# One memset instead of two behind some gathers, and three merge operations ahead of the last sums: a sort-based GraphSAGE aggregation on one core

## The chip, the cores and the metric

The kernel runs on one core of a Trainium2 chip. A core has TensorE (PE: matrix products, and PEld, the weight loads beside them), VectorE (DVE), ScalarE (ACT), GpSimd (POOL) and SyncE (SP), which run their own instruction streams and wait for each other through semaphores. 16 DMA engines move data between HBM and the core's memory. The metric is the device time of one launch in microseconds (us). Of the kernel before, three runs gave 2193.62, 2194.74 and 2198.55 us, so its median is 2194.74 us.

## The reference

A graph of 12,500 nodes and 800,000 edges is given as two index lists. Every node has 64 features. The features of the edges' sources are added up onto the edges' destinations, the sum is scaled by the inverse in-degree, and two 64x64 products give the output:

```python
N, deg, D = 12500, 64, 64
E = N * deg

def reference(x, src, dst, deg_inv, w_self, w_neigh):
    nsum = _segment_sum(x[src], dst, N)      # tgt.at[dst].add(x[src])
    h_neigh = nsum * deg_inv[:, None]
    return x @ w_self + h_neigh @ w_neigh
```

`src` and `dst` are drawn at random, so the gather and the scatter are irregular. The kernel turns them into a sort and dense products.

## The kernel before, in words

Every edge becomes one 32-bit key: a bucket number (block of 144 destinations x block of 128 sources), then the destination and the source inside the block. The program then goes through these stages.

1. **Sort in each partition.** Each of the 128 partitions sorts its 6,250 keys on DVE (line 228), and the result `runs` is written to memory as `d1`. This takes the first quarter of the time.
2. **First run gathers.** The buckets are given to 128 + 128 rows: part 0 (41 buckets a row) and part 1 (27 a row). `find_rows` counts on ACT and DVE where each row's run begins in each partition, and `gather_runs` (line 468) fetches, for each of the 128 partitions p, one short run per row: an indirect DMA on POOL's queue, with `start[part]` as the indices. There are 128 such gathers for part 0 (`range(128)`), then 104 for part 1 (`FIRST = 104`), and later 24 more. Behind every gather stands `pause()` (line 382): two memsets on POOL of a scratch tile `pad` that nothing reads then.
3. **Merges.** `merge_runs` merges the gathered runs of a row on DVE by min and max operations (lines 280 and 292; ACT copies what stays, line 276). Part 0 is merged in groups of 16, 16, 32 and 64 runs, so the last group's first operation needs gathers 64 to 127. `merge_last` (lines 309 to 324) makes the last level of part 0.
4. **Counts.** `find_buckets(0)` counts on ACT, for each of the 41 buckets of a row, how many keys lie below it (line 605). When the last count is there, two small DVE operations (lines 621 and 622, the "last sums") make the start of every bucket's window.
5. **Bucket gathers.** `gather_buckets(0)` makes the index of each window (line 637, DVE) and fetches it (line 626, POOL, an indirect DMA into `v`), with a `pause()` behind each of the 41. Behind them POOL runs the last 24 run gathers of part 1.
6. **Decode.** `decode_buckets(0)` splits the gathered keys, four buckets at a time, into source and destination (lines 673 to 678 on DVE, 683 and 687 on ACT, a transpose on PE).
7. **Nodes.** For every bucket, DVE makes a one-hot matrix of the sources (`ohs`, line 780, from a DMA `slb` that spreads the indices over the partitions) and one of the destinations (`ohd`, line 783). PE multiplies (`ct`, line 808), ACT, and from the second half on DVE too, copies the product out of PSUM (`xg`, lines 818 and 816), and PE adds up with `ohd` (`acc`, line 864). 1,066 tiles of 8 buckets go through this. Part 1's merges, its find, gather and decode run between the tiles.

The order on every engine is written by hand: the whole of `after_sort` and `sums_and_merge` stands in one `manual_schedule` block, and instructions are issued on each engine in the order in which Python emits them. Merges of part 1 are a generator whose steps are pulled one by one. Steps are pulled where the program wants DVE to have work: two bucket counts per merge step while the counts last (`while counts:` in `sums_and_merge`), then some 8 us of merges by an estimate, then 2.8 us of them per decode step, and in the nodes stage 0.32 us per tile.

Of the kernel before, what the change touches and what calls it, by code (L numbers as in the profile page):

```python
# [31 lines left out]
KPRS = (41, 27)  # L32
# [21 lines left out]
SPLIT = 2560  # L54
SIGMA = 6.0
LOWER = 2240
LAG = 4
OCT = 7

# [47 lines left out]
WIN = Windows()  # L107
NLOWER = sum(lo + n <= LOWER for lo, n in WIN.w2[0])
NC1 = len(WIN.w1)
# [189 lines left out]
def merge_last(nc, src, oth, off, rstride, ln, lout, split, done):  # L299


    plan, na, nb, alone = merge_plan(ln, lout)

    def at(t, z, n):
        return view(t, off + z, [[2, n]])

    for op, n, z in ((OP.min, na, 0), (OP.max, nb, 1)):
        x, y = (view(src, off + o, [[1, n]]) for o in (0, rstride))
        nc.vector.tensor_tensor(at(oth, z, n), x, y, op=op)
        yield n / 0.96 + 125  # L310
    for a, e in alone:
        z = 2 * (a % ln) + a // ln
        nc.scalar.activation(at(src, z, e - a), at(oth, z, e - a), AF.Copy)
    edge = [split]
    for (first, *_), (then, *_) in zip(plan[-2::-1], plan[:0:-1]):
        edge.insert(0, edge[0] + max(2 * first - 1, 2 * then - 1))
    for upper in range(2):
        cur, nxt = oth, src
        for (k, lo, *ends), e in zip(plan, edge):
            for op, end, z in zip((OP.min, OP.max), ends, (1, 2 * k)):  # L320
                i = max(0, -((z - e) // 2))
                a, b = (max(lo, i), end) if upper else (lo, min(end, i))
                if b > a:
                    nc.vector.tensor_tensor(at(nxt, 2 * a + z, b - a), at(cur, 2 * a + 1, b - a),
                                            at(cur, 2 * (a + k), b - a), op=op)
                yield (b - a) / 0.96 + 125
            cur, nxt = nxt, cur
        if not upper:
            done(cur)


def flat(ap, n):
    return bass.AP(tensor=ap.tensor, offset=ap.offset, ap=[[1, n], [1, 1]])


class Kernel:
# [39 lines left out]
        nc.gpsimd.iota(self.wide, pattern=[[1, OCT * HN]], base=0, channel_multiplier=0,  # L376
                       allow_small_or_imprecise_dtypes=True)

    def pause(self):

        for _ in range(2):
            self.nc.gpsimd.memset(self.pad, 0.0)  # L382

    def make_keys(self, pool, keys):
# [78 lines left out]
    def gather_runs(self, part, u, runs):  # L463
        nc = self.nc
        nr, w = ROWS[part], LENS[part][0]
        src = flat(self.d1, 128 * PITCH1)
        for p in runs:
            nc.gpsimd.indirect_dma_start(  # L468
                out=u[:nr, p * w:(p + 1) * w], out_offset=None, in_=src,
                in_offset=bass.IndirectOffsetOnAxis(ap=self.start[part][:nr, p:p + 1], axis=0))  # L470
            self.pause()

    def merge_runs(self, part, u, pong, sizes):

# [7 lines left out]
        def round_(level, off, rstride, nruns):  # L482
            src = bufs[par[level]]
            args = nc, src, bufs[1 - par[level]], off, rstride
            if part == 0 and level == 6:
                def done(rows):
                    self.rows, self.lower = rows, True
                yield from merge_last(*args, lens[level], lens[level + 1], LOWER, done)
            else:
# [120 lines left out]
    def find_buckets(self, part):  # L610


        nc = self.nc
        acc = self.keep.tile([128, KPRS[part]], F32, name=f"acc2_{part}")
        nc.sync.dma_start(self.d2[part][:, SIDE:SIDE + LOWER], self.rows[:, :LOWER])
        for k in range(KPRS[part]):
            if k == NLOWER:
                nc.sync.dma_start(self.d2[part][:, SIDE + LOWER:SIDE + LROW[part]], self.rows[:, LOWER:LROW[part]])
            self.count_below(part, k, acc)
            yield k  # L620
        nc.vector.tensor_tensor(acc, acc, self.c2[part][:, 3], op=OP.mult)
        nc.vector.tensor_tensor(acc, acc, self.c2[part][:, 4], op=OP.add)
        self.first = acc
# [6 lines left out]
    def gather_buckets(self, part, vp):  # L630

        nc = self.nc
        kpr = KPRS[part]
        self.v = vp.tile([128, kpr, 2 * SIDE], I32, name="v")
        ix = self.keep.tile([128, kpr], U32, name=f"ix2_{part}")
        for k in range(kpr):
            nc.vector.tensor_scalar(ix[:, k:k + 1], self.first[:, k:k + 1], 0.0, None, op0=OP.max)
            self.gather_window(part, k, ix)
            self.pause()

    def find_and_gather(self, part, vp):

# [5 lines left out]
        ix = self.keep.tile([128, kpr], U32, name=f"ix2_{part}")  # L648
        for k in range(kpr + LAG):
            if k == 1:  # L650
                self.store_rows(part, nc.scalar)
            if k < kpr:
                self.count_below(part, k, acc)
            if k >= LAG:
                g = k - LAG
                nc.scalar.activation(ix[:, g:g + 1], acc[:, g:g + 1], AF.Relu, bias=self.c2[part][:, 4, g:g + 1])
# [504 lines left out]
```

## Time and profile before

| what | before |
|---|---|
| median of the runs shown | 2194.74 us (2193.62 to 2198.55) |
| profiled execution | 2187.01 us, span 2185.2 us |
| busy: PE, DVE, ACT, POOL | 1031.3, 1998.6, 1261.8, 651.4 us |
| line 228, in-partition sort on DVE | 228.5 + 227.3 us |
| lines 808 and 864, products on PE | 602.7 + 411.1 us |
| line 468, run gathers on POOL | 256, 339.1 us busy |
| line 382, pauses on POOL | 594 memsets, 114.7 us busy |

The profiled execution is one run, 7.7 us below the median of the others. The page shows busy time per engine, the program's lines with their counts and mean durations, and what each engine waited for. A timeline row gives start, duration, engine, line, operation, the tiles written and read, and in brackets the idle time just before with the releaser that ended it. An engine's busy share over the whole span says little here, because the stages follow each other with different engines in the lead. DVE leads up to about 1090 us, and from there PE, DVE and ACT are all nearly full.

### The profile page before, as it was taken

Reading aid. Unit: us, or ns where it says so; the run is one execution under the profiler, and the core shown is the slowest. Engines: PE = TensorE matmul, PEld = TensorE weight load, DVE = VectorE, ACT = ScalarE, POOL = GpSimd, SP = SyncE. Lnnn points to the kernel's source line nnn. Section 1 sums busy time; section 2 is a strip of 40 time slices with the busy share of each in tenths; the row PEclk is TensorE's granted clock in tenths of the full one; section 3 lists DMA queues with packets and bytes.
Section 4 is the critical chain, followed back from the end, with each engine's and each line's share of the span. In section 5 each row is a group of like instructions: output and inputs, shape, how many; then the busy total and the mean of one; then the engine's idle time right before and its main releaser. Section 6 shows DMA issues by size and latency. Waiting matters only on the chain.

```text
span 2185.2 us, 59787 instructions
## 1 busy us (share of the span) xinstructions
PE 1031.3 (47%) x26089; PEld 888.8 (41%) x26089; DVE 1998.6 (91%) x2198; ACT 1261.8 (58%) x1747; POOL 651.4 (30%) x1020
## 2 busy tenths in 40 slices
PE   0150000000000000000089998999987989999987
PEld 0140000000000000000077887877776878788776
DVE  7999999999899599988999999999998888889887
ACT  6470000019500000062289999999997888888886
POOL 1000000001888888977861100101431010010010
PEclk9965555555555555555589999999999999999999
DMA  5140000000000000012188777778876887777784
GB/s 159 37 107 6 0 0 0 0 24 39 21 19 20 16 14 13 10 53 57 50 293 280 272 284 265 270 270 278 310 271 219 291 272 291 263 279 291 277 280 163
DMA packets 111311, 331.46 MB, mean 152 GB/s; under 512 B 56528, under 2 KB 64656, under 8 KB 110400
## 3 DMA queue, kind: packets, MB, share of 16 engines
q1 hardware_dynamic: 90352, 306.14, 38.9%
q0 software_dynamic: 14864, 19.18, 4.8%
q8 instruction: 206, 3.38, 0.6%
q10 hardware_dynamic: 5824, 2.24, 0.4%
q14 instruction: 65, 0.53, 0.1%
HBM read 308.39 MB, written 19.10 MB: 150 GB/s over the span
## 4 chain that ended last, share of the span: by engine, by line
PE 35%; DVE 28%; POOL 18%; issue 10%; ACT 7%; DMA 3%; another core or an unknown queue 0%; ACTq 0%; SPq 0%; DVEq 0%; POOLq 0%
PE ct L808 20%; PE acc L864 13%; POOL u L468 13%; DVE a L228 10%; DVE b L228 9%; POOL pad L382 4%; ACT xg L818 2%; ACT junka L449 2%; DVE ohd L783 2%; DVE ohs L780 2%; DVE u L292 1%; DMA v<-d,ix 1%; PE po L932 1%; POOL v L626 1%; PE acc L869 1%
## 5 line engine op out<-in xcount | busy, mean ns | idle before, releaser
L818 ACT ACTIVATE xg<-ct 128x1024 f16<-128x1024 f32 (+1 forms) x994 | 937.8, 1082 | 102.6 <-PE ct L808 83.4
L808 PE MATMUL ct<-xh,ohs 128*128 128x128 f16 x8526 | 602.7, 222 | 49.9 <-DVE ohs L780 20.1
L808 PEld LDWEIGHTS <-ohs 128*128 128x128 f16 x8526 | 498.6, 99 | 96.6 <-issue 35.8
L468 POOL DMA_INDIRECT u<-d,ix x256 | 339.1, 1325 | 533.7 <-ACT junka L449 491.2
L292 DVE TENSOR_TENSOR u<-u 128x256 f32<-128x256 f32 (+47 forms) x494 | 453.3, 949 | 23.7 <-ACT u L276 15.8
L864 PE MATMUL acc<-ohd,xg 64*128 64x72 f16 x17052 | 411.1, 194 | 57.0 <-issue 42.2
L864 PEld LDWEIGHTS <-xg 64*128 64x128 f16 x17052 | 324.6, 95 | 133.0 <-issue 52.5
L780 DVE TENSOR_SCALAR ohs<-slb,pidx 128x3584 f16<-128x3584 bf16 x305 | 350.5, 1149 | 24.3 <-PE ct L808 18.9
L783 DVE TENSOR_TENSOR ohd<-iota,dlT 128x2016 f16<-128x2016 bf16 x305 | 366.6, 1202 | 0.0
L693 PE MATMUL tr<-idb,l 128*128 128x128 bf16 x68 | 9.0, 271 | 493.4 <-ACT l L687 488.5
L228 DVE TENSOR_TENSOR a<-b 128x106 f32<-128x106 f32 (+31 forms) x114 | 228.5, 2056 | 1.2
L228 DVE TENSOR_TENSOR b<-a 128x106 f32<-128x106 f32 (+36 forms) x112 | 227.3, 2080 | 1.0
L276 ACT ACTIVATE u<-u 128x256 f32<-128x256 f32 (+15 forms) x94 | 46.8, 577 | 310.2 <-DVE u L280 309.0
L693 PEld LDWEIGHTS <-l 128*128 128x128 bf16 x68 | 5.6, 117 | 496.9 <-ACT l L687 492.3
L458 PE MATMUL stp<-idf,st 128*128 128x128 f32 x2 | 0.9, 446 | 416.0 <-DVE st L456 416.0
L940 POOL DMA_DIRECT2D out<-o x24 | 24.7, 1029 | 547.5 <-DVE o L939 518.9
L458 PEld LDWEIGHTS stp<-idf,st 128*128 128x128 f32 x2 | 0.4, 182 | 416.5 <-issue 416.5
L845 POOL DMA_INDIRECT lx<-xt,lxi x44 | 78.9, 1793 | 300.0 <-PE ct L808 161.0
L816 DVE CAST xg<-ct 128x1024 f16<-128x1024 f32 x75 | 91.7, 1223 | 57.1 <-PE ct L808 57.0
L231 ACT ACTIVATE a<-b 128x106 f32<-128x106 f32 (+12 forms) x20 | 13.5, 708 | 205.2 <-DVE b L228 198.6
L382 POOL MEMSET pad<- 128x89 f32 x594 | 114.7, 193 | 17.5
L280 DVE TENSOR_TENSOR u<-u 128x512 f32<-128x512 f32 (+21 forms) x68 | 75.8, 1145 | 26.5 <-DMA u<-d,ix 22.8
(135 smaller groups left out, 858.2 us busy)
## 6 DMA issues: line engine op xcount, KB each, us to landing
slb<-sl SPq DMA_DIRECT2D x305, 896.0 KB
u<-d,ix POOLq DMA_INDIRECT x256
xt<-xh SPq DMA_DIRECT2D x1, 3136.0 KB
own<-os SPq DMA_DIRECT2D x12, 256.0 KB
fo<-own SPq DMA_DIRECT2D x24, 126.0 KB
out<-o POOLq DMA_DIRECT2D x24, 126.0 KB
rd<-dst SPq DMA_DIRECT2D x4, 521.0 KB
rs<-src SPq DMA_DIRECT2D x4, 521.0 KB
```

The costliest lines, as they stand in the source:

```text
L228: nc.vector.tensor_tensor(view(dst, lo + sh, [[st, g], [1, l]]), x, y, op=op)
L280: nc.vector.tensor_tensor(at(oth, to, n), x, y, op=op)
L292: nc.vector.tensor_tensor(to, at(cur, ln + lo, n), at(cur, lo + k, n), op=op)
L382: self.nc.gpsimd.memset(self.pad, 0.0)
L468: nc.gpsimd.indirect_dma_start(out=u[:nr, p * w:(p + 1) * w], out_offset=None, in_=src, in_offset=bass.IndirectOffsetOnAxis(ap=self.start[ ...
L780: nc.vector.tensor_scalar(s.rearrange("p c s -> p (c s)"), b, self.pidx[:, :1], None, op0=OP.is_equal)
L783: nc.vector.tensor_tensor(d, self.iota[:, None].to_broadcast([128, 14, HN, 2]), ix, op=OP.is_equal)
L808: nc.tensor.matmul(ct[:, i * 128:(i + 1) * 128], cols[i][0], self.xh[:, (b0 + i) % NB].rearrange("p a f -> p (a f)"), start=True, stop=True)
L816: nc.vector.tensor_copy(xg[:, :cnt * 128], ct[:, :cnt * 128])
L818: nc.scalar.activation(xg[:, :cnt * 128], ct[:, :cnt * 128], AF.Copy)
L845: nc.gpsimd.indirect_dma_start(out=x, out_offset=None, in_=self.xt, in_offset=bass.IndirectOffsetOnAxis(ap=ix.bitcast(U32), axis=0))
L864: nc.tensor.matmul(acc[h][:, db % OCT * HN:(db % OCT + 1) * HN], xg[r, i * 128:(i + 1) * 128], d[r], start=db % OCT == 0 and sb == 0, stop ...
```

## The change

`pause` takes a number of memsets. Gathers 32 to 127 of part 0 and the 41 bucket gathers get one memset instead of two; gathers 0 to 31 of part 0 and all gathers of part 1 keep two. And `find_buckets` yields six more times between the last count and the last sums. Since two steps of it are pulled per merge step, three merge operations of part 1 come to stand ahead of the two sums in DVE's order, and all later merge operations stand three steps earlier in the program.

```diff
+CLOSE = 32
+BEHIND = 6
...
-    def pause(self):
-
-        for _ in range(2):
+    def pause(self, n):
+
+        for _ in range(n):
             self.nc.gpsimd.memset(self.pad, 0.0)
...
                 in_offset=bass.IndirectOffsetOnAxis(ap=self.start[part][:nr, p:p + 1], axis=0))
-            self.pause()
+            self.pause(1 if part == 0 and p >= CLOSE else 2)
...
             self.count_below(part, k, acc)
             yield k
+        for _ in range(BEHIND):
+            yield KPRS[part]
         nc.vector.tensor_tensor(acc, acc, self.c2[part][:, 3], op=OP.mult)
         nc.vector.tensor_tensor(acc, acc, self.c2[part][:, 4], op=OP.add)
...
             self.gather_window(part, k, ix)
-            self.pause()
+            self.pause(1)
```

On POOL nothing moves: 137 of its 594 memsets are gone, 96 behind gathers 32 to 127 of part 0 and 41 behind the bucket gathers. In the changed kernel lines up to `find_buckets` lie two lower (468 becomes 470, 382 becomes 384), later ones four.

DVE's order around the last sums (`acc`), which wait for ACT's last count, before:

```order
L292 TENSOR_TENSOR u<-u 128x32x40
L621 TENSOR_TENSOR acc_0_2196<-acc_0_2196,c_0_69 128x41
L622 TENSOR_TENSOR acc_0_2196<-acc_0_2196,c_0_69 128x41
L637 TENSOR_SCALAR ix_0_2318<-acc_0_2196 128x1 x41
L292 TENSOR_TENSOR u<-u 128x32x39
L292 TENSOR_TENSOR u<-u 128x32x40
L292 TENSOR_TENSOR u<-u 128x32x39
L280 TENSOR_TENSOR u<-u 128x16x80 x2
```

and with the change:

```order
L294 TENSOR_TENSOR u<-u 128x32x40
L294 TENSOR_TENSOR u<-u 128x32x39
L294 TENSOR_TENSOR u<-u 128x32x40
L294 TENSOR_TENSOR u<-u 128x32x39
L625 TENSOR_TENSOR acc_0_2100<-acc_0_2100,c_0_69 128x41
L626 TENSOR_TENSOR acc_0_2100<-acc_0_2100,c_0_69 128x41
L641 TENSOR_SCALAR ix_0_2225<-acc_0_2100 128x1 x41
L282 TENSOR_TENSOR u<-u 128x16x80 x2
```

The three merge operations that stood behind the 41 index operations now stand ahead of the sums.

In the nodes stage DVE alternates one-hot pairs (`ohs`, `ohd`) with merge operations of part 1. Its second group of 64 runs begins with the operation of 128x32x48. Before, it stands behind 13 one-hot pairs:

```order
L280 TENSOR_TENSOR u<-u 128x780
L292 TENSOR_TENSOR u<-u 128x485 x2
L292 TENSOR_TENSOR u<-u 128x689
L780 TENSOR_SCALAR ohs<-slb,pidx 128x3584
L783 TENSOR_TENSOR ohd<-iota,dlT 128x2016
```

These are the rows ahead of the first pair. With the change four later merge operations stand there, and the 128x32x48 stands behind 8 pairs:

```order
L294 TENSOR_TENSOR u<-u 128x733
L294 TENSOR_TENSOR u<-u 128x749
L294 TENSOR_TENSOR u<-u 128x733
L294 TENSOR_TENSOR u<-u 128x741
L784 TENSOR_SCALAR ohs<-slb,pidx 128x3584
L787 TENSOR_TENSOR ohd<-iota,dlT 128x2016
```

So the second group, which reads what the last 24 run gathers fetch, begins five one-hot pairs earlier.

## The prediction

> **What bounds the kernel now.** I read the busy times first, then a table by stage, then who waited for whom on DVE.
>
> ```profile
> PE 1031.3 (47%) x26089; PEld 888.8 (41%) x26089; DVE 1998.6 (91%) x2198; ACT 1261.8 (58%) x1747; POOL 651.4 (30%) x1020
> ...
> 530.00:735.00 205.00, 0.89 (x2) 0.36 (x2) 185.74 (x384) 58.41 (x210) 170.99 (x343) 0.50 0.08 19
> 735.00:757.00 22.00, 0.00 (x0) 0.00 (x0) 0.11 (x1) 0.00 (x0) 18.64 (x43) 0.50 0.09 21
> ...
> 975.00:1097.00 122.00, 7.69 (x54) 4.87 (x55) 109.72 (x183) 26.96 (x48) 94.22 (x169) 0.50 0.22 62
> 1097.00:1300.00 203.00, 190.51 (x4918) 164.01 (x4915) 200.24 (x222) 194.98 (x220) 48.78 (x36) 0.97 0.80 280
> ```
>
> In the rows of stretches the columns are start and end, length, then busy us of PE, PEld, DVE, ACT and POOL, the granted clock, the DMA share and GB/s. Up to 1097 us DVE carries the program and PE does almost nothing. From there PE, DVE and ACT are all over 93% busy, so that stage has a length of its own (2185 - 1097 = 1088 us) and follows whatever starts it. Between 735 and 757 every engine but POOL stands. What DVE waits for in the first half:
>
> ```profile
> DVE u L280 <- DMA u<-d,ix: 22.8, 1, 22.8
> DVE ohs L780 <- PE ct L808: 18.9, 23, 2.1
> ...
> DVE acc L621 <- ACT junk L605: 6.7, 1, 6.7
> DVE v L673 <- DMA v<-d,ix: 6.1, 6, 1.8
> ```
>
> The columns are the sum in us, how often, and the longest. The change is aimed at rows one, three and four: 22.8 + 6.7 + 6.1 = 35.6 us at most.
>
> **The run gathers (22.8 us).** The hole stands between these rows:
>
> ```profile
> 640.71 1.54 POOL L468 DMA_INDIRECT u<-d,ix  x1 [0.15 <-issue]
> ...
> 714.46 19.67 DVE L292 TENSOR_TENSOR u<-u 128x849 f32<-128x849 f32 x16 [1.73 <-ACT u L276]
> ...
> 738.34 0.42 POOL L382 MEMSET pad<- 128x89 f32 x2
> 738.92 0.95 POOL L468 DMA_INDIRECT u<-d,ix  x1 [0.15 <-issue]
> ...
> 754.19 0.95 POOL L468 DMA_INDIRECT u<-d,ix  x1 [0.15 <-issue]
> ...
> 756.89 4.49 DVE L280 TENSOR_TENSOR u<-u 128x2048 f32<-128x2048 f32 x2 [22.76 <-DMA u<-d,ix]
> ```
>
> DVE is through with three groups of runs at 714.46 + 19.67 = 734.13. The fourth needs gather 127, which POOL begins at 754.19 and ends at 755.14. DVE goes on 1.75 us later, when the data have landed. With DVE idle a gather takes 0.95 us, its two memsets 0.42 and the gap 0.15 (a pitch of 1.53). What one memset costs:
>
> ```profile
> 699.96 0.19 POOL L382 MEMSET pad<- 128x89 f32 x1
> ```
>
> So 0.42 - 0.19 = 0.23 us go per gather, and 0.34 instead of 0.57 us lie between two gathers. For 96 gathers that is 96 x 0.23 = 22 us, almost the whole hole, if POOL waits for nothing else. It does wait while DVE works:
>
> ```profile
> 721.71 1.93 POOL L468 DMA_INDIRECT u<-d,ix  x1 [1.55 <-issue]
> 722.73 7.68 DVE L292 TENSOR_TENSOR u<-u 128x1085 f32<-128x1085 f32 x6
> 724.04 1.30 DVE L292 TENSOR_TENSOR u<-u 128x1093 f32<-128x1093 f32 x1
> 724.22 1.95 POOL L468 DMA_INDIRECT u<-d,ix  x1 [0.15 <-issue]
> ...
> 726.75 1.95 POOL L468 DMA_INDIRECT u<-d,ix  x1 [0.15 <-issue]
> ...
> L468 POOL DMA_INDIRECT u<-d,ix x50 | 63.5, 1269 | 9.1 <-issue 9.1
> L382 POOL MEMSET pad<- 128x89 f32 x100 | 18.1, 181 | 2.9
> ```
>
> The gather that starts at 724.22 meets the DVE operation that ends at 724.04 + 1.30 = 725.34, and itself ends at 724.22 + 1.95 = 726.17, 0.83 later. A gather thus ends 0.95 us after its start or 0.83 us after the end of the DVE operation that it met, whichever is later. Memsets are not held up (181 ns each). The gathers 64 to 113 (x50) take 1.27 us on average for that reason. In the stretch of long operations POOL and DVE are locked in step: one gather for two operations (726.75 - 724.22 = 2.53 = 2 x 1.27). From 0.83 us behind an operation's end it is 0.34 us to the next start, 1.17 together, which is just short of one operation (7.68 / 6 = 1.28). So there the step should fall from two operations to one; with 0.57 us it is 1.40, over one. That is what decides this term.
>
> I went through all recorded starts and ends of DVE's operations with this rule, gather by gather from 32 on, with 0.34 us between gathers. (With 0.57 it gives back the recorded starts up to the 1.55 us gap at 721.71.) Gather 64 then starts at 635.0 and not at 640.71, and the last one at 735.4 and not at 754.19. The saving is **18.8 us**: 22 by count, less 5 of longer waits (the last 14 gathers no longer have an idle DVE), and 1.4 because the issue gap, which follows the number of instructions issued, falls behind gather 127. If the gap stays, it is 17.5. With 0.33 us between gathers the same gives 20.0, with 0.36 us 16.1. The low bound is that every gather which waited for DVE gives its saving back as a longer wait: 42 of the 96 took the bare 0.95 us (counted in the timeline), so 42 x 0.23 = 10 us. The high bound is the hole, 22.8. I take 18.8; DVE still waits 4 us.
>
> The Trainium skill ("SBUF — State Buffer", section "Who interferes with whom") says that a DVE instruction with two SBUF inputs contends with a GpSimd instruction that reads SBUF, not with one that only writes it. The trace agrees: gathers (which read their indices) wait, memsets do not. The page adds that the first to start holds the port for its whole instruction and the other fully blocks; what that would make of the time is the third rival.
>
> **The three merge operations (6.7 us).** They are these x3, and they fill a wait:
>
> ```profile
> 974.63 0.20 DVE L621 TENSOR_TENSOR acc<-acc,c 128x41 f32<-128x41 f32 x1 [6.71 <-ACT junk L605]
> 977.60 4.35 DVE L292 TENSOR_TENSOR u<-u 128x1248 f32<-128x1248 f32 x3
> ```
>
> 4.35 of 6.71 us are filled, and the sums still wait 2.4 us for ACT's last count; the bucket gathers start no sooner and no later against that count. Behind them the program pulls the same number of merge steps as before (8 us, then 2.8 per decode step), only later ones. So this part does not bring the nodes stage forward. It takes 4.35 us of DVE work out of it. PE, DVE and ACT share the lead there, so I book 0, with 4.35 as the best case.
>
> **The bucket gathers (6.1 us).**
>
> ```profile
> L626 POOL DMA_INDIRECT v<-d,ix x41 | 50.4, 1230 | 27.7 <-issue 14.1 <-DVE ix L637 7.2 <-DVE v L673 2.7
> 983.72 1.98 POOL L626 DMA_INDIRECT v<-d,ix  x1 [0.53 <-issue]
> 987.66 0.69 DVE L673 TENSOR_TENSOR v<-v,c 128x512 int32<-128x512 int32 x1 [1.80 <-DMA v<-d,ix]
> ```
>
> 41 gathers fill 976 to 1066 us, 2.2 us each, of which 0.95 lie between two gathers (0.42 + 0.53). DVE works off four in about 8 us, so it waits for them: 6.1 us in six waits, the first of 1.80. With 0.23 less per gather the last one ends 41 x 0.23 = 9.4 us sooner, less what DVE's operations hold up. By the same rule and the changed order of DVE, none of the six waits is left; with the old order the first would keep 1.5. I take **5.5 us**, bounds 0 and 6.1.
>
> **The nodes stage.** Its start moves by 18.8 + 5.5. One thing in it does not move along: the second group of part 1 now stands behind 8 one-hot pairs and not 13, and needs the last 24 run gathers.
>
> ```profile
> 1094.47 1.15 DVE L780 TENSOR_SCALAR ohs<-slb,pidx 128x3584 f16<-128x3584 bf16 x1 [1.59 <-DMA slb<-sl]
> ...
> 1114.54 10.58 POOL L468 DMA_INDIRECT u<-d,ix  x1 [0.15 <-issue]
> ...
> 1120.37 0.91 DVE L292 TENSOR_TENSOR u<-u 128x738 f32<-128x738 f32 x1
> ...
> 1128.83 0.95 POOL L468 DMA_INDIRECT u<-d,ix  x1 [0.15 <-issue]
> ...
> 1138.22 1.75 DVE L280 TENSOR_TENSOR u<-u 128x1536 f32<-128x1536 f32 x1
> ...
> L468 POOL DMA_INDIRECT u<-d,ix x9 | 24.8, 2753 | 1.4 <-issue 1.4
> ```
>
> Before, the last gather ends at 1129.8 and lands some 2 us later, 37 us behind the first one-hot; the merge needs it at 1138.22, 44 us behind. Eight pairs end at about 1120, so the need now comes 26 us behind the first one-hot. The last nine gathers, caught between one-hots, took 36 us with their memsets, 4 each; with the bucket gathers done 4 us sooner against the first one-hot, about two fewer are left, and the last lands near 30. DVE would stand about 4 us. The waits of `ohs` for PE (18.9 us in 23 waits, quoted above) show that DVE runs ahead by its one-hot buffers, 28 buckets each, so PE has work for that long. I book 0, and up to 5 as a cost.
>
> **Sum.** Against the profiled execution: 2187.0 - 18.8 - 5.5 = 2162.7 us. That execution was 7.7 us below the median, so the forecast for the median is 2194.7 - 24.3 = **2170.4 us**, 1.1% faster.
>
> **Rivals.**
>
> 1. *The waits swallow the pause.* The step of 1.17 us does not fit under DVE's operations, because one memset alone has a longer tail than the 0.15 us that stand behind two. Then only the unhindered gathers save: 10 us, and half of the bucket waits, 3. That gives 2182. For it speaks how near 1.17 and 1.28 are; against it, that the row of a single memset and the gap are constant to 0.01 us. Chance 0.10.
> 2. *The last run gathers come too late* (slower). Two mechanisms meet at one place, the 128x32x48 operation: DVE runs in order, and one-hots queue behind it. Every more gather that is caught for 10.58 us as at 1114.54 adds 10 us of standing DVE to the 4. It turns the sign from the point where the last landing lies 26 + 24 = 50 us behind the first one-hot, two more such blocks; with three, 2170.4 + 4 + 31.5 = 2206. Before, nine gathers met one such block, so three in seven are unlikely. With one more it is 2170.4 + 14 = 2185. Chance 0.06 for one block, 0.02 for the slower case.
> 3. *The gather holds DVE.* If the gather were first and blocked DVE for its 0.95 us, the 14 gathers that now run beside an idle DVE would be moved into its work and cost 14 x 0.95 = 13 us there. That gives 2170.4 + 13 = 2184. Against it: three gathers start within the six DVE operations from 722.73 on, and these take 1.28 us each with no idle time. Chance 0.04.
> 4. *DVE's relief counts.* If DVE leads the nodes stage (200.24 of 203 us busy), the 4.35 us come on top: 2166. Chance 0.10.
>
> **How the numbers follow.** The forecast has the other 0.68. Its own range, from 16.1 and 20.0 in the first term, 4 to 6 in the second and up to 5 lost in the nodes stage, is 2168 to 2180. A range of **2161 to 2183** takes in rival 4 with a hole that closes fully, and rival 1. What a measurement of this kernel can tell from no change is about 0.2%, 4.4 us. All cases but the slow end of rival 2 are faster by more; I keep some chance for what no row shows. Faster 0.94, within 0.04, slower 0.02.
>
> **What would show it.** DVE's wait at line 280 (282 in the changed kernel) for `u` falls from 22.8 to about 4 us, and gathers in the stretch of long operations come every 1.3 us and not 2.5. If they still come every 2.5, rival 1 holds. The wait of `acc` falls to 2.4 us and the six waits of `v` are gone or one short one is left. The first `ohs` starts near 1070 and the nodes stage keeps its length; a wait of DVE at line 282 for `u` behind the eighth pair, longer than 5 us, is rival 2. DVE operations of 1,090 elements longer than 1.3 us would be rival 3.

## The result and the profile after

The changed kernel takes 2164.48 us (median of 4 runs, 2159.76 to 2167.47) beside 2196.64 us for the kernel before (4 runs, 2193.62 to 2200.02). The ratio is 0.9851, with a 95% interval of 0.9827 to 0.9876: 1.5% faster, where 1.1% was forecast. The profiled execution took 2167.47 us with a span of 2165.7 us.

Busy times and the table by stage of the changed kernel. The columns of a stretch are start and end, length, then the busy us of PE, PEld, DVE, ACT and POOL, the granted clock, the DMA share and GB/s:

```profile
PE 1031.7 (48%) x26089; PEld 889.5 (41%) x26089; DVE 1998.0 (92%) x2199; ACT 1261.7 (58%) x1746; POOL 610.7 (28%) x883
...
530.00:735.00 205.00, 0.90 (x2) 0.37 (x2) 186.50 (x390) 59.76 (x214) 173.14 (x288) 0.50 0.10 21
735.00:757.00 22.00, 0.00 (x0) 0.00 (x0) 20.35 (x13) 2.00 (x2) 19.72 (x32) 0.50 0.07 13
...
1069.00:1272.00 203.00, 184.40 (x4728) 158.51 (x4728) 195.10 (x218) 188.59 (x214) 21.40 (x15) 0.97 0.79 273
```

POOL's busy time fell by 40.7 us (651.4 - 610.7), that of every other engine changed by less than 1 us. The stretch from 735 to 757, in which DVE was busy for 0.11 us, now has 20.35 us of DVE work. What DVE waits for (sum, how often, longest):

```profile
DVE ohs L784 <- PE ct L812: 21.2, 21, 4.6
...
DVE u L282 <- POOL pad L384: 2.9, 1, 2.9
DVE acc L625 <- ACT junk L607: 2.5, 1, 2.5
DVE u L282 <- issue: 1.4, 1, 1.4
```

Of the three waits at which the change was aimed, the 22.8 us are 1.4, the 6.7 us are 2.5, and the 6.1 us of `v` have no row any more. The 2.9 us for `pad` at line 282 are old: before, the same wait took 3.0 us. The place of the large hole, in the timeline:

```profile
715.26 20.03 DVE L294 TENSOR_TENSOR u<-u 128x849 f32<-128x849 f32 x16 [1.73 <-ACT u L278]
...
719.72 0.95 POOL L470 DMA_INDIRECT u<-d,ix  x1 [0.16 <-issue]
720.66 0.20 POOL L384 MEMSET pad<- 128x89 f32 x1
721.02 0.94 POOL L470 DMA_INDIRECT u<-d,ix  x1 [0.16 <-issue]
...
733.98 0.94 POOL L470 DMA_INDIRECT u<-d,ix  x1 [0.16 <-issue]
...
736.71 4.49 DVE L282 TENSOR_TENSOR u<-u 128x2048 f32<-128x2048 f32 x2 [1.41 <-issue]
```

In DVE's long operations gathers now come every 1.30 us (721.02 - 719.72), one for each operation, and the last of part 0 starts at 733.98 instead of 754.19. DVE still stands 1.41 us: it starts at 736.71, 1.79 us behind the end of that gather, as it did before (1.75), so this is the time until the data land.

### The profile page after: what moved, and what is told of

Its sections match the earlier page's. It is cut to its first block, busy times and chain, and to the rows that moved or that the text cites. A ratio compares the mean times of both kernels' runs of the same rounds, so it can differ in the third digit from the quotient of the medians.

```text
span 2165.7 us, 59651 instructions
## 1 busy us (share of the span) xinstructions
PE 1031.7 (48%) x26089; PEld 889.5 (41%) x26089; DVE 1998.0 (92%) x2199; ACT 1261.7 (58%) x1746; POOL 610.7 (28%) x883
## 4 chain that ended last, share of the span: by engine, by line
PE 37%; DVE 36%; POOL 10%; issue 8%; ACT 6%; DMA 2%; SPq 1%; DVEq 0%; ACTq 0%; POOLq 0%
PE ct L812 21%; PE acc L868 14%; DVE a L230 9%; DVE b L230 9%; DVE u L294 7%; POOL u L470 7%; ACT junka L451 2%; DVE u L326 2%; DVE ohd L787 2%; POOL pad L384 2%; POOL v L630 2%; DVE ohs L784 2%; ACT xg L822 1%; DVE u L282 1%; PE po L936 1%
## 5 line engine op out<-in xcount | busy, mean ns | idle before, releaser
L470 POOL DMA_INDIRECT u<-d,ix x256 | 326.1, 1274 | 533.2 <-ACT junka L451 491.9
L849 POOL DMA_INDIRECT lx<-xt,lxi x44 | 72.4, 1645 | 330.2 <-DVE lxi L847 176.5
L630 POOL DMA_INDIRECT v<-d,ix x68 | 90.0, 1323 | 58.5 <-DMA d<-u 24.0
L233 ACT ACTIVATE b<-a 128x1024 f32<-128x1024 f32 (+19 forms) x32 | 22.9, 770 | 126.7 <-DVE a L230 126.7
```

The lines of the kernel that those rows point to most:

```text
L470: nc.gpsimd.indirect_dma_start(out=u[:nr, p * w:(p + 1) * w], out_offset=None, in_=src, in_offset=bass.IndirectOffsetOnAxis(ap=self.start[ ...
L630: self.nc.gpsimd.indirect_dma_start(out=self.v[:, k].bitcast(F32), out_offset=None, in_=flat(self.d2[part], 128 * PITCH2[part]), in_offset ...
L849: nc.gpsimd.indirect_dma_start(out=x, out_offset=None, in_=self.xt, in_offset=bass.IndirectOffsetOnAxis(ap=ix.bitcast(U32), axis=0))
```

## The experiments

**Stages.** For every kernel the trace gives the length of four stages: from the first sum of `find_rows(0)` (tile `st`) to the first operation of the fourth group (the gather stage), from there to the last sums (`acc`), from there to the first one-hot, and from there to PE's last product (the nodes stage). The two rows of the gather stage in the changed kernel and the one of `st` in the kernel before:

```profile
537.31 0.29 DVE L457 TENSOR_TENSOR st<-acc,c 128x128 f32<-128x128 f32 x1 [0.67 <-ACT junka L451]
736.71 4.49 DVE L282 TENSOR_TENSOR u<-u 128x2048 f32<-128x2048 f32 x2 [1.41 <-issue]
```
```profile
535.88 0.29 DVE L455 TENSOR_TENSOR st<-acc,c 128x128 f32<-128x128 f32 x1 [0.67 <-ACT junka L449]
```

So the gather stage is 736.71 - 537.31 = 199.4 us, before 756.89 - 535.88 = 221.0. The other entries are made from starts in the same way:

| kernel | gather stage | to `acc` | `acc` to first one-hot | nodes stage |
|---|---|---|---|---|
| before | 221.0 | 217.7 | 119.8 | 1084.8 |
| the change | 199.4 | 217.7 | 112.5 | 1093.1 |
| run gathers alone | 200.4 | 217.7 | 119.7 | 1077.9 |
| bucket gathers alone | 220.5 | 217.7 | 113.2 | 1078.7 |
| merges alone | 220.7 | 217.8 | 119.1 | 1087.6 |
| both pauses, no merges | 200.6 | 217.7 | 113.3 | 1075.9 |
| the change, again | 199.3 | 217.7 | 112.4 | 1088.6 |
| both pauses, again | 200.4 | 217.8 | 113.2 | 1078.6 |
| five merges | 200.5 | 218.2 | 113.7 | 1080.3 |
| one memset in all of part 0 | 231.4 | 217.8 | 113.2 | 1076.0 |
| one long memset, gathers 0 to 31 | 197.6 | 217.8 | 113.3 | 1088.6 |
| one middle memset, gathers 0 to 31 | 201.1 | 217.8 | 113.2 | 1095.0 |
| no memset, gathers 32 to 127 and buckets | 197.9 | 217.8 | 112.7 | 1086.2 |
| one memset in part 1 too | 200.7 | 217.5 | 113.1 | 1091.3 |

The first three stages repeat within 1 us for one arrangement. The nodes stage does not: among kernels whose merges stand as before, one profiled execution each, it takes 1076 to 1095 us. Part of that may be the chip and not the execution. The last four rows were run on another chip than the other experiments, and the kernel before took 2193.32 us on that chip and 2187.3 us on the first one. With the merges unmoved the nodes stage took 1076 to 1079 us on the first chip and 1086 to 1095 us on the other. But on one chip, too, the executions of the kernel before spread from 2175.49 to 2202.81 us. So small effects are read from the first three stages, and the nodes stage only from medians taken beside each other.

**Each part alone.** The edits, against the changed kernel:

```diff
 # run gathers alone
-BEHIND = 6
+BEHIND = 0
-            self.pause(1)          # behind a bucket gather
+            self.pause(2)
 # bucket gathers alone
-BEHIND = 6
+BEHIND = 0
-            self.pause(1 if part == 0 and p >= CLOSE else 2)
+            self.pause(2)
 # merges alone: both pauses back to 2
 # both pauses, no merges
-BEHIND = 6
+BEHIND = 0
```

> Only gathers 32 to 127 of part 0 have one memset; the bucket gathers keep two, and no merge operations are moved. By the theory that the part-0 gathers set the start of the last merge group and everything behind moves along: DVE's wait for the last run gather falls from 22.8 to about 1.4 us, the first one-hot starts 20 to 21 us earlier than the 1094.5 us of the profile before, the wait of the sums for ACT stays 6.7 us and the six waits for the bucket gathers stay about 6 us. Time 20 to 21 us below before, ratio 0.990. By the rival that the nodes stage gives a part back: less than 15 us.

> Only the 41 bucket gathers have one memset. Theory: the six waits of the key splits on DVE, 6.1 us, are gone except the first, and the gathers come every 1.6 to 1.9 us instead of 2.2; the first one-hot starts 4.5 to 6 us earlier than before; the waits of 22.8 and 6.7 us stay. Time 4.5 to 6 us below before, ratio 0.9975. Rival (the waits were hidden by ACT, PE or the slb transfer): the waits go and the first one-hot stays within 1 us of 1094.5.

> Only the three merge operations stand ahead of the last sums; all pauses have two memsets. By the forecast's booking (it brings the nodes stage forward by nothing, and PE, DVE and ACT share the lead there): the wait of the sums falls from 6.7 to 2.4 us, the first one-hot starts within 1.5 us of 1094.5, and the time is within 2 us of before. By the rival that DVE's relief of 4.35 us counts in the nodes stage: 4 to 5 us below before, ratio 0.998.

> Both pauses shortened, without the three merge operations. If the three edits add up: the sum of the two runs before this, 25 to 27 us below before, ratio 0.988, and 0 to 5 us behind the whole change. If the moved merges are worth 4.35 us in the nodes stage, the whole change (0.985) is 4 to 5 us faster than this one; if they are worth nothing, the two are equal. In the bucket stage the first split should still wait about 1.5 us.

Measured, beside 2187.26 us for the kernel before: run gathers alone 2168.38 us, ratio 0.9913 [0.9884, 0.9942]; bucket gathers alone 2176.05, 0.9949 [0.9929, 0.9970]; merges alone 2185.43, 0.9991 [0.9962, 1.0021]; both pauses 2158.79, 0.9874 [0.9841, 0.9908]. In the stages the run gathers are worth 20.6 us (221.0 - 200.4), the bucket gathers 6.6 (119.8 - 113.2), the merges 0.7 (119.8 - 119.1), and each part moves only its own one of the first three stages, apart from 0.5 us. The pauses carry the gain. Two expectations were missed. In time the bucket gathers alone gave 11 us (6.6 to 15.5 by the interval) and not 4.5 to 6. And with both pauses and no moved merges, the first split was to keep a wait of 1.5 us; in that trace, as in the one of the bucket gathers alone, DVE has no wait for `v` left ahead of the nodes stage.

The merges alone show the one danger that the forecast saw in the nodes stage. In the trace of that kernel:

```profile
1114.35 6.73 POOL L470 DMA_INDIRECT u<-d,ix  x1 [0.15 <-issue]
...
1121.65 0.95 POOL L470 DMA_INDIRECT u<-d,ix  x1 [0.15 <-issue]
```
```profile
1119.06 1.19 DVE L787 TENSOR_TENSOR ohd<-iota,dlT 128x2016 f16<-128x2016 bf16 x1
1125.94 1.76 DVE L282 TENSOR_TENSOR u<-u 128x1536 f32<-128x1536 f32 x1 [5.70 <-DMA u<-d,ix]
```

The 128x32x48 operation (1,536 elements) behind the eighth pair stands 5.70 us for the last run gathers, because they still run among the one-hots. In the changed kernel they do not:

```profile
1066.97 1.15 DVE L784 TENSOR_SCALAR ohs<-slb,pidx 128x3584 f16<-128x3584 bf16 x1 [1.24 <-DMA slb<-sl]
...
1093.73 1.74 DVE L282 TENSOR_TENSOR u<-u 128x1536 f32<-128x1536 f32 x1
```
```profile
1071.47 1.66 POOL L470 DMA_INDIRECT u<-d,ix  x1 [0.16 <-issue]
```

The shorter bucket pause lets the last gather start 4.5 us behind the first one-hot (1071.47 - 1066.97), 22 us ahead of its use.

**Do the merges cost time in the nodes stage?** The two kernels with three moved merges had the longest nodes stages of the runs so far (1093.1 and 1087.6 us against 1075.9 to 1084.8). ACT's copies of 128x16x32 then stand close ahead of the copies `g<-acc` at the end of the first seven blocks, which could hold PE. So the change and its version without the merges were timed side by side, with a version of five merges (`BEHIND = 10`).

> The changed kernel once more, beside the kernel with both pauses shortened and no merges moved. The runs so far gave 2164.5 us for the one and 2158.8 us for the other, from different comparisons whose own reference differs by 9 us. Theory A (the three moved merges cost time in the nodes stage: ACT's copies of 128x16x32 then stand just ahead of the copies g<-acc at the end of the first seven blocks, and PE waits): the changed kernel is 5 to 12 us slower than the kernel without moved merges, and its profile shows a wait of DVE for ACT's copy of 2 us or more and a nodes stage over 1085 us. Theory B (the moved merges do nothing, 1076 to 1093 us for the nodes stage is chance between executions): the two are within 4 us of each other, and the length of the nodes stage does not go with the moved merges.

> Both pauses shortened, no merges moved, once more. Theory A: 0.987 of the kernel before, 5 to 12 us faster than the changed kernel beside it. Theory B: within 4 us of it.

> Five merge operations ahead of the last sums instead of three. The wait of the sums for ACT's count is 2.4 us in the changed kernel; two more merges of 1.45 us overfill it, so the sums and the bucket gathers come 0.5 us later. Theory A: the copies 128x16x32 on ACT then stand right behind the copies 128x32x32, two more places ahead of g<-acc, and the time changes by several us against the changed kernel in either direction. Theory B: within 4 us of the changed kernel.

Measured, beside 2187.34 us for the kernel before: the change 2152.53 us, 0.9849 [0.9815, 0.9883]; without the merges 2158.11, 0.9871 [0.9830, 0.9913]; five merges 2156.69, 0.9867 [0.9835, 0.9899]. The medians of the first two are 5.6 us apart, but in favour of the change, where theory A wanted 5 to 12 us the other way. That is beyond the 4 us that theory B allowed, but the runs spread from 2148.6 to 2162.4 us for the one and from 2142.1 to 2166.2 us for the other, and the intervals of the ratios overlap: these runs do not tell the three apart. Both signs that theory A named for the profile did come: the nodes stage of the change, again, took 1088.6 us, and DVE waits once in it for ACT's copy, 3.7 us, the longest wait of this row:

```profile
DVE u L294 <- ACT u L278: 17.1, 13, 3.7
```

The other two kernels with three moved merges have such a wait in the nodes stage of 2.8 us (the change) and 5.4 us (merges alone). The kernels with the old order and the one with five merges have none above 1.52 us. So the wait is real. The long nodes stage is not shown to go with it, since the profiled execution took 2161.75 us, 9.2 us above the median of its six. If the first three stages repeat, the nodes stage of the median execution takes an estimated 1088.6 - 9.2 = 1079 us, and without the merges 1078.6 + (2158.11 - 2154.40) = 1082 us. The price that theory A put on the merges does not show in the times. What the merges are worth is in the stages, 0.7 to 0.8 us (113.2 - 112.4). With five, the sums wait for DVE's own merges, and the 0.8 us are lost again (113.7).

**One memset behind the first 32 gathers too.** The change leaves them two. The edit: `CLOSE = 0`, no moved merges.

> One memset behind all 128 run gathers of part 0 (32 more than in the change) and behind the bucket gathers, no merges moved. The changed kernel still waits 2.9 us for POOL in its first merge groups and 1.4 us at the fourth. If a memset's 0.23 us and the event between two memsets are spared there as well, these 4.3 us go: 2 to 5 us less than the kernel with both pauses shortened. If the first merges have other limits (the sort's last output, the index sums), nothing changes: within 2 us.

Measured: 2198.61 us, ratio 1.0053 [1.0023, 1.0083]. Neither expectation held: this is 40 us slower than both pauses beside it, and slower than the kernel before. The gather stage grew from 200.4 to 231.4 us. These 31 us do not cover the 40; the traced execution took 2182.91 us, the least of the twelve, and what the slower ones lost besides was not traced. Groups of the stretch from 537 to 620 us, first with two memsets there, then with one (busy us, mean ns | idle us ahead, and what ended it):

```profile
L451 ACT ACTIVATE junka<-b,c 128x3 bf16<-128x3 f32 (+34 forms) x73 | 30.2, 414 | 2.3
L453 DVE TENSOR_SCALAR_CACHE_REDUCE junkd<-b,c 128x214 bf16<-128x214 f32 (+51 forms) x54 | 21.5, 399 | 1.9
```
```profile
L451 ACT ACTIVATE junka<-b,c 128x3 bf16<-128x3 f32 (+34 forms) x73 | 30.1, 413 | 32.7 <-remote 14.6 <-ACT junka L451 14.1 <-issue 2.5
L453 DVE TENSOR_SCALAR_CACHE_REDUCE junkd<-b,c 128x214 bf16<-128x214 f32 (+51 forms) x54 | 21.6, 399 | 29.8 <-remote 15.9 <-DVE junkd L453 10.2 <-issue 2.4
```

These are the counts of `find_rows(1)`, which ACT and DVE run while the first gathers of part 0 go out. Each count takes as long as before, but some 30 us of standing lie between them on both engines. They stand in steps:

```profile
574.98 0.36 DVE L453 TENSOR_SCALAR_CACHE_REDUCE junkd<-b,c 128x141 bf16<-128x141 f32 x1 [2.43 <-remote]
577.78 0.36 DVE L453 TENSOR_SCALAR_CACHE_REDUCE junkd<-b,c 128x139 bf16<-128x139 f32 x1 [2.43 <-remote]
...
582.68 0.35 DVE L453 TENSOR_SCALAR_CACHE_REDUCE junkd<-b,c 128x132 bf16<-128x132 f32 x1 [1.74 <-remote]
584.12 0.34 DVE L453 TENSOR_SCALAR_CACHE_REDUCE junkd<-b,c 128x128 bf16<-128x128 f32 x1 [1.08 <-DVE junkd L453]
```
```profile
574.28 0.41 ACT L451 ACTIVATE junka<-b,c 128x131 bf16<-128x131 f32 x1 [2.31 <-remote]
577.07 0.41 ACT L451 ACTIVATE junka<-b,c 128x126 bf16<-128x126 f32 x1 [2.29 <-remote]
```

Starts of one engine lie 2.80 or 1.44 us apart, and the two engines 0.70 us (574.98 - 574.28): near multiples of 0.70 us on both, as if they were served in turn. POOL stands too: four of its memsets waited 0.85 to 1.19 us there. Two runs put the first 32 gathers at other distances, by one memset of another length in place of the two:

```diff
-BEHIND = 6
+BEHIND = 0
...
+        self.wpad = keep.tile([128, 304], FH, name="wpad")     # 197 in the second
...
+    def wait_once(self):
+        self.nc.gpsimd.memset(self.wpad, 0.0)
...
-            self.pause(1 if part == 0 and p >= CLOSE else 2)
+            if part == 0 and p < CLOSE:
+                self.wait_once()
+            else:
+                self.pause(1 if part == 0 else 2)
```

> Both pauses shortened, no merges moved, and behind gathers 0 to 31 of part 0 one memset of 128x304 in place of the two of 128x89. With one short memset there (the run before) ACT's and DVE's counts of part 1's runs waited in steps of 0.70 us and the gather stage took 231 us instead of 200. Theory A (the time between two gathers decides: 1.30 us was too dense, 1.53 is not): a memset of 304 columns takes about 0.4 us by the rows of 89 and 150 columns (0.17 and 0.23 us), so gathers come about every 1.5 us again, the counts do not wait, the stage takes 200 to 202 us and the time is within 5 us of the kernel with two memsets there. Theory B (it is the number of memsets or the event between them, not the time): the counts wait as before, the stage takes about 231 us and the time is 30 to 40 us longer.

> The same with one memset of 128x197 there, so that gathers come about every 1.4 us. Theory A with a gradual limit: the counts wait for a part of the time that they waited at 1.30 us, and the gather stage takes 205 to 225 us. Theory A with the limit below 1.4 us: no waits, 200 to 202 us. Theory B: 231 us.

The memset of 304 columns took 0.37 us and that of 197 columns 0.28 us, so gathers came every 1.47 and 1.39 us. Measured, beside 2193.32 us: 2167.48 us, 0.9900 [0.9860, 0.9939], and 2167.84, 0.9890 [0.9839, 0.9941]. The same groups, long, then middle:

```profile
L455 ACT ACTIVATE junka<-b,c 128x3 bf16<-128x3 f32 (+34 forms) x73 | 30.2, 414 | 2.3
L457 DVE TENSOR_SCALAR_CACHE_REDUCE junkd<-b,c 128x214 bf16<-128x214 f32 (+51 forms) x54 | 21.6, 399 | 1.9
```
```profile
L455 ACT ACTIVATE junka<-b,c 128x3 bf16<-128x3 f32 (+33 forms) x72 | 29.7, 412 | 6.6 <-ACT junka L455 4.6
L457 DVE TENSOR_SCALAR_CACHE_REDUCE junkd<-b,c 128x214 bf16<-128x214 f32 (+51 forms) x54 | 21.6, 399 | 3.9 <-DVE junkd L457 2.1
```

The gather stage of the first was to take 200 to 202 us and took 197.6, that of the second was to take 205 to 225 us under a gradual limit and took 201.1. The kernel with two memsets there was not timed beside them, so the 5 us of theory A were not tested. It is the distance and not the number of memsets (theory B is out): at 1.47 us the counts stand no more than at 1.53 (2.3 and 1.9 us), at 1.39 a little (6.6 and 3.9), at 1.30 for 32.7 and 29.8 us. The limit is steep: from 1.39 to 1.30 us the gather stage grows from 201.1 to 231.4 us. Each distance was traced once, and that of 1.30 us on another chip than those of 1.39 and 1.47. Gathers 32 to 127 at 1.30 us do no such harm in the change. They run behind the counts: the last count starts at 580.30, gather 31 at 588.33. What is short is not settled: in the stretch from 550 to 600 us the queues that bring instructions moved one packet with the stall and two without it, and no engine or queue was full. Every execution timed here has its span and clock from such records, so a part played by the recording can't be excluded either.

**No memset, and one in part 1.**

```diff
 # no memset (BEHIND = 0 in both)
-            self.pause(1 if part == 0 and p >= CLOSE else 2)
+            self.pause(0 if part == 0 and p >= CLOSE else 2)
-            self.pause(1)          # behind a bucket gather
+            self.pause(0)
 # one memset in part 1 too
-            self.pause(1 if part == 0 and p >= CLOSE else 2)
+            self.pause(1 if part == 1 or p >= CLOSE else 2)
```

> No memset behind gathers 32 to 127 of part 0 and behind the bucket gathers, two behind the others, no merges moved. Forecast's rule (a gather ends 0.95 us after its start or 0.83 us after the end of the DVE operation that it met): gathers that meet no DVE operation come every 1.1 us instead of 1.30, those in long operations cannot come faster than one operation of 1.28 us, so the last gather of part 0 ends a little sooner and only the 1.4 us wait at the fourth group goes: 0 to 3 us less than with one memset. Rival (engines starve when gathers come every 1.1 to 1.3 us while ACT and DVE issue many instructions): here ACT issues few instructions while gathers 32 to 127 run, but gathers 32 to 45 still meet the end of the counts, and DVE would show waits in steps of 0.70 us; 5 to 30 us more.

> One memset instead of two also behind all 128 gathers of part 1, beside the short pauses, no merges moved. Nothing waits for these gathers except the second group of part 1 in the nodes stage, so the stages ahead keep their lengths (200.4, 217.7 and 113.3 us) and the time stays within 4 us. Rival (gathers every 1.3 us starve ACT's bucket counts and DVE's merges, which run beside the first 104 of them): the stage of 217.7 us grows by 5 us or more.

Measured: 2158.14 us, 0.9845 [0.9802, 0.9889], and 2163.95, 0.9863 [0.9816, 0.9909]. Without a memset:

```profile
721.13 0.94 POOL L470 DMA_INDIRECT u<-d,ix  x1 [0.30 <-issue]
722.38 0.98 POOL L470 DMA_INDIRECT u<-d,ix  x1 [0.30 <-issue]
...
733.99 4.49 DVE L282 TENSOR_TENSOR u<-u 128x2048 f32<-128x2048 f32 x2
```

Two gathers then stand 0.30 us apart, against 0.35 with one memset (0.19 + 0.16) and 0.57 with two. So the first memset costs 0.05 us of distance and the second 0.22. The hole is gone altogether and the gather stage is 2.5 us shorter than with one memset (200.4 to 197.9), in the rule's own range of 0 to 3 us. No count stands, but that tests nothing: here too the last count starts at 579.12, ahead of gather 32, against what the expectation said. One memset in part 1 changes none of the first three stages by more than 0.3 us, as the forecast's side had it. For ACT's bucket counts the rival was not tested either: with one memset the 104 gathers start up to 896.31, and the bucket counts begin at 912.24. DVE's merges do run beside these gathers; 34 of the 103 steps between them were at most 1.33 us, and DVE's idle time ahead of its merges in the stretch from 735 to 900 us stayed at 7.4 us. The intervals of the change (0.9851, 0.9849), five merges, no memset and one in part 1 overlap: no version tried is shown to beat the change.

## Why the prediction was right, point by point

**Run gathers: right, 2.8 us too little.** Forecast 18.8 us within 10 to 22.8; the gather stage lost 21.6. The rule for a gather that meets a DVE operation held with one exception (below): gather 64 was to start 5.7 us sooner and did so by 5.8, counted from `st`, and one gather for each long operation came true. The step that was mis-sized is the "5 of longer waits". The 96 gathers and their memsets, before and after:

```profile
L468 POOL DMA_INDIRECT u<-d,ix x96 | 110.3, 1149 | 16.2 <-issue 16.2
L382 POOL MEMSET pad<- 128x89 f32 x192 | 34.8, 181 | 5.6
```
```profile
L470 POOL DMA_INDIRECT u<-d,ix x96 | 111.6, 1163 | 15.4 <-issue 15.4
L384 POOL MEMSET pad<- 128x89 f32 x97 | 18.8, 194 | 0.1
```

Memsets and the idle time ahead of them fell by 34.8 + 5.6 - 18.8 - 0.1 = 21.5 us, as the 22 by count said. The gathers themselves grew by 1.3 us (111.6 - 110.3), not by 5. The last 14, which no longer have an idle DVE, show where: they took 13.3 us before and 14.8 with the change, since 12 of them still took the bare 0.95. The rule gives 17.2 us for them: gone through once more with the operations of before and 0.34 us between gathers, it gives back the 635.0 and 735.4 of the forecast if it holds a gather only from 0.04 us behind an operation's start on, and three gathers that start just later than that are then held for 2.1 us each. In the trace none is held among the operations from 719.76 on; what happens there instead is the next point. Rival 1 (the waits swallow the pause) is out.

Two smaller points of this term. Its parts, 22 - 5 + 1.4, add up to 18.4 and not 18.8. And no run shows that the issue gap of 1.55 us "follows the number of instructions issued" and falls behind gather 127: wherever the pauses of part 0 are shortened, the gap ahead of gather 109 is gone and does not come back at a later gather of part 0, while the second one, ahead of gather 215, stays where it is in all but one of these kernels, with 96 to 192 memsets fewer ahead of it. That the 1.4 us were saved is right; the reason given is not.

**Rival 3, the gather holds DVE: there, but tiny.** One group of DVE's long operations, before and after:

```profile
L292 DVE TENSOR_TENSOR u<-u 128x1086 f32<-128x1086 f32 x2 | 2.6, 1285 | 0.0
```
```profile
L294 DVE TENSOR_TENSOR u<-u 128x1086 f32<-128x1086 f32 x2 | 2.7, 1344 | 0.0
```

These operations take 0.06 us longer, and the whole stretch of 16 takes 20.03 instead of 19.67 us. Only six of the 16 are longer, and it is the order of the starts that tells which. Two neighbours of the changed kernel:

```profile
720.99 1.35 DVE L294 TENSOR_TENSOR u<-u 128x1085 f32<-128x1085 f32 x1
721.02 0.94 POOL L470 DMA_INDIRECT u<-d,ix  x1 [0.16 <-issue]
```
```profile
722.31 0.95 POOL L470 DMA_INDIRECT u<-d,ix  x1 [0.16 <-issue]
722.38 1.31 DVE L294 TENSOR_TENSOR u<-u 128x1101 f32<-128x1101 f32 x1
```

The gather at 721.02 starts 0.03 us behind its operation. It still takes the bare 0.94 us, and the operation takes 1.35 us where an operation of this size took 1.28 before. This is the exception to the rule: DVE gives way a little, and the gather keeps its place in the step. The gather at 722.31 starts 0.07 us ahead of its operation, and the operation takes 1.31 us, as it did before. Before, the gather at 726.75 started 0.17 us behind its operation and was held for its whole length (1.95 us). So none of the gathers in this stretch costs DVE more than 0.07 of its 0.95 us. The Trainium skill ("SBUF — State Buffer", section "Summary: rules for kernel authors") says that, when a DVE instruction has two SBUF inputs and the GpSimd operation reads SBUF, the second one to issue fully blocks until the first finishes. The gather that starts 0.17 us late agrees; the two in the rows above do not, so here the measurement decides against a full block.

**Bucket gathers: nearly right in time, wrong in the gap.** Forecast 5.5 us, bounds 0 and 6.1; the stage from `acc` to the first one-hot lost 6.6 with this part alone, 0.5 above the upper bound. All waits of `v` are gone, as the rule said, and with the old order of DVE too, where it had left 1.5 us. But the gap fell further than the forecast's 0.23 us:

```profile
1020.83 0.20 POOL L384 MEMSET pad<- 128x89 f32 x1
1021.18 1.67 POOL L630 DMA_INDIRECT v<-d,ix  x1 [0.16 <-DVE u L294]
```

With two memsets 0.42 + 0.53 us lay between two bucket gathers, now 0.19 + 0.16: 0.60 less for each. The forecast kept the 0.53 us as fixed; it went with the second memset. DVE then had the lead in that stage (107.4 of 113.3 us busy with both pauses), so nearly all of it beyond the waits found no taker there. That the time came out near 5.5 is owed to this limit and not to the gap that was forecast.

**Merges: right.** The wait of the sums was to fall to 2.4 us:

```profile
954.44 0.20 DVE L625 TENSOR_TENSOR acc<-acc,c 128x41 f32<-128x41 f32 x1 [2.46 <-ACT junk L607]
```

They were booked at 0 and give 0.7 to 0.8 us ahead of the nodes stage. Rival 4 (their 4.35 us count in full) is neither shown nor excluded: the median with them is 5.6 us lower, within the spread of the runs, and alone they gave 0.9991 [0.9962, 1.0021], which holds both nothing and 4.35 us.

**Nodes stage: the 4 us of standing did not come.** The forecast let the last 24 gathers follow only 4 us sooner against the first one-hot. They came far sooner, since the gap of the bucket gathers fell by 0.60 us and not by 0.23, and the merge found its data. Within the forecast this is luck: the gap that was taken too large would have left the 4 us, which were named and booked at 0. Rival 2's mechanism is real: merges alone show it with 5.70 us, close to the 4 of the forecast.

**The sum.** Stages ahead of the nodes give 21.6 + 7.3 = 28.9 us, against 24.3 booked. The median fell by 32.2 us, and the interval of the ratio reaches from 27 to 38 us, so the 28.9 us account for it within what these runs can tell. The time lies within the range of 2161 to 2183 us, 5.9 us below the forecast: 2.8 us of this are the run gathers, 1.8 the bucket gathers and merges together, and the rest is not told from the spread of the nodes stage.

## What to carry to other kernels

Where gathers come from a queue one by one, work out their step against the operations of the engine that holds them up: cutting 0.23 us from a pause was worth a whole operation each where it brought the step below one, and it is the row of the long operations that says so. A pause with no visible use can protect other engines: before one is shortened, look at which engines issue many short instructions beside it, and shorten it only where there are none. Where executions of one kernel spread by 27 us, as here, read effects of a few us from stages that repeat, and compare the rest only between runs of one chip.

## What the runs showed of the hardware that was not expected

- Gathers of 128 rows every 1.30 us hold up ACT and DVE while these issue counts of about 0.5 us each: about 30 us of standing on each, in steps of near 0.70 us. At 1.39 us it is a few us, at 1.47 no more than at 1.53. The cause is open.
- A gather and a DVE operation that start within 0.07 us of each other run side by side: the gather takes 0.95 us, and the operation 0 to 0.07 us more. A gather that starts 0.17 us behind an operation is held until 0.83 us behind its end.
- The distance between two indirect DMAs on POOL is 0.30 us with nothing between them, 0.35 with one memset of 0.19 us and 0.57 with two. Behind bucket gathers a second memset cost 0.60 us, more than twice its own 0.2.
